# Attention and MLP in one kernel: the subtraction of a weight's low words one step later, the copy of the reciprocals at a step's end

## The chip, the cores and the metric

The kernel runs on one core of one Trainium2 chip. A core has engines that run side by side, each with its own order of instructions: TensorE (PE: matrix products and transposes, into PSUM), VectorE (DVE), ScalarE (ACT), GpSimd (POOL) and SyncE (SP, which here issues transfers). They meet only at semaphores, and an engine does its instructions in the order in which they were written. The metric is the device time of one execution in microseconds (us), as a median of several runs.

## What is computed

Attention over 4 batches, 8 heads, 576 positions and 64 channels, with a bias made from the distance of two positions by a small network, and then a two-layer MLP with a gate on the result. Cut to what matters:

```python
def _attn_ref(q, k, v, w1, b1, w2):
    scores = scale * np.matmul(q, k.transpose(0, 1, 3, 2))
    ...
    h = np.maximum(x @ w1 + b1, 0.0)
    bias = h @ w2
    scores = scores + bias.transpose(2, 0, 1)[None, :, :, :]
    scores = scores - np.max(scores, axis=-1, keepdims=True)
    attn = np.exp(scores)
    attn = attn / (np.sum(attn, axis=-1, keepdims=True) + 1e-09)
    return np.matmul(attn, v).astype(np.float32)

def _moe_ref(x, w_in, w_out):
    h = x @ w_in
    sp = np.where(h > 20.0, h, np.log1p(np.exp(np.minimum(h, 20.0))))
    g = h * np.tanh(sp)
    return (g @ w_out).astype(np.float32)
```

x is 2304 x 512, w_in 512 x 2048 and w_out 2048 x 512. The MLP's weights arrive as 64-bit floating point numbers, two 32-bit words each.

## The kernel before, in words

Three stages follow each other. First the bias is made and written to DRAM (to about 66 us). Then the attention loop, to about 330 us. Then the MLP, to the end.

**The attention loop** goes over 16 pairs of heads (a pair is two heads of one batch), and in each over five chunks of query rows, in the order 0, 1, 4, 2, 3. That makes 80 steps, n = 0 to 79; x = n mod 5 is the step in its pair. Steps 0, 1, 3 and 4 of a pair hold 128 rows of both heads; step 2 holds the last 64 rows of both heads in one tile, and so half the work on DVE and ACT. `step(n)` writes, in this order:

- `scores(n)` (L217, PE): three products for each score tile, for precision (high by high, high by low, low by high). There are two score tiles in PSUM, and a step of 128 rows uses both.
- `add_bias(n)` (L231, DVE): adds the bias to the scores, writes them to SBUF and takes the minimum of the negated row, in one instruction for each score tile; then a short read of the minimum. This frees the score tile. The text calls it the bias-and-minimum.
- `exps(n, 0)` (L246, ACT): the exponential of the first half, with its row sums.
- `transposes(n - 2)`: PE transposes the exponentials of two steps ago into tiles of PSUM (L289, L292), of which there are three in a ring; ACT copies them to SBUF, two main parts (L290) and a tail (L296). Step 1 of a pair also transposes the reciprocals of the sums of the pair before, into the tail's PSUM tile (L295), and `store_reciprocals` copies them to SBUF on DVE (L258) and stores them by SP (L259).
- `exps(n, 1)` (ACT), then `ahead(n)`: loads for later pairs, on SP and POOL.
- `reciprocals` in step 0, for the pair that has just ended (L251, L252, DVE).
- `split(n)`: DVE's side work. In step 2 it splits q and k of the next pair into high and low words (L184). And it prepares one of the MLP's weights, in a cycle of four steps: scale the high word (L112 or L114), shift the low word (L120, which also issues the next load), merge (L127), and put in the sign (L134). With the sign goes `split_weights`: ACT casts the weight to the form that PE takes (L143), and DVE subtracts the cast from the weight for its low words (L144). A cycle of four steps against pairs of five puts the sign in steps 4, 3, 2, 1, 0 in turn; 16 of the 32 weights are prepared so, from n = 6 to n = 69, the rest in the MLP.
- `pv_duo`: parts of the products of the transposed exponentials with v (L322, L326, PE), in one PSUM tile. When a group of rows is done, DVE copies it out (L329: in steps 1 and 3), and the next group's products wait for that copy. SP writes it to DRAM. The text calls L329 the product copy.

No scheduler reorders this: the order of the calls is the order on each engine.

Of the kernel before, what the change touches and what calls it, by code (L numbers as in the profile page):

```python
# [44 lines left out]
def kernel(ctx: ExitStack, tc, qk, v, wb, w2, w_in, w_out, psia, psi4, rinv, eye, out):  # L45
    nc = tc.nc
    pe, dve, act, pool, sp = nc.tensor, nc.vector, nc.scalar, nc.gpsimd, nc.sync
# [39 lines left out]
    todo, w64, half, w32 = list(order), [], [], []  # L87
# [17 lines left out]
    def scale_high(eng):  # L105

        job, w = w64.pop(0)
        high = convp.tile([P, 512], F32, name="high", bufs=1)  # L110
        if eng is act:
            act.mul(high, w.bitcast(F32)[:, :, 1], 2.0 ** -112)  # L112
        else:
            dve.tensor_scalar(high, w.bitcast(F32)[:, :, 1], 2.0 ** -112, None, op0=ALU.mult)  # L114
        half.append((job, w, high))
# [15 lines left out]
    def sign():  # L131
        job, high, c = half.pop(0)
        cu = c.bitcast(U32)
        dve.scalar_tensor_tensor(cu, high.bitcast(U32), 0x80000000, cu,  # L134
                                 op0=ALU.bitwise_and, op1=ALU.bitwise_or)
        w32.append((job, c))

    def split_weights(eng):
        job, c = w32.pop(0)
        if job not in w_hi:  # L140
            w_hi[job] = ring.tile([P, 512], F32R, name="wh{}{}{}".format(*job))
            w_lo[job] = ring.tile([P, 512], F32R, name="wl{}{}{}".format(*job))
        act.copy(w_hi[job], c)  # L143
        eng.tensor_tensor(w_lo[job], c, w_hi[job].bitcast(F32), op=ALU.subtract)  # L144


# [34 lines left out]
    def split_qk(i):  # L181

        lo = hip.tile([P, QW], F32R, name="qklo")
        dve.tensor_tensor(lo, qk_raw.pop(i), qk_hi[i].bitcast(F32), op=ALU.subtract)  # L184
        qk_lo[i] = lo
# [22 lines left out]
    def scores(n):  # L208
        i, c = steps[n]
        hi, lo = qk_hi[i], qk_lo[i]  # L210
        live[n] = [s_ps.tile([P, 2, 512], F32, name="s") for _ in range(2 if c < 4 else 1)]
        for k, (stat, mov) in enumerate(((hi, hi), (hi, lo), (lo, hi))):
            for j in range(2):
                for h in range(2 if c < 4 else 1):
                    rows = slice(h * 64, h * 64 + 64) if c < 4 else slice(0, P)
                    k0 = KO + (0 if h else 64) + j * SH
                    pe.matmul(live[n][h][:, j, :SH], stat[rows, c * P:(c + 1) * P], mov[rows, k0:k0 + SH],  # L217
                              start=(k == 0), stop=(k == 2))

    def add_bias(n):  # L220

        i, c = steps[n]
        bt = bias_t[i // B, c]
        m = st.tile([P, 2], F32, name="m")
        if c < 4:
            pt = pp.tile([P, 2 * S], F32, name="pt")
        else:
            pt = p4p.tile([P, 640], F32, name="pt4")[:, :S]
        for u, s in enumerate(live[n]):
            sl = slice(u * S, (u + 1) * S)  # L230
            dve.tensor_tensor_reduce(  # L231
                out=halves(pt[:, sl]), in0=s[:, :, :SH], in1=halves(bt[:, sl]),
                scale=-0.125, scalar=BIG, op0=ALU.add, op1=ALU.min, accum_out=m[:, u:u + 1])
        live[n] = (pt, m)

    def exps(n, u):

        i, c = steps[n]
        if u == 1 and c == 4:
            return  # L240
        if i not in sums:
            sums[i] = st.tile([P, 9], F32, name="sums", bufs=3)
        pt, m = live[n]
        ps = pt[:, u * S:(u + 1) * S]
        k = 4 * u + c if c < 4 else 8
        act.activation(ps, ps, AF.Exp, bias=m[:, u:u + 1], scale=-1.0, accum_out=sums[i][:, k:k + 1])  # L246

    def reciprocals(i):

        r = sums.pop(i)  # L250
        dve.tensor_scalar(r, r, 1e-9, None, op0=ALU.add)  # L251
        dve.reciprocal(r, r)  # L252
        return r

    def store_reciprocals(i, r, tp):
        hp, b = divmod(i, B)
        rt = rt_first.pop() if rt_first else rt_tile()
        dve.tensor_copy(rt, tp[0:9, P:2 * P])  # L258
        sp.dma_start(out=r_d[b][hp], in_=rt)  # L259

    def pt_tiles(grp):
        w = 256 if grp == 0 else 320
        main = ptp.tile([P, 2, 4, w], F32, name=f"main{grp}")
        tail = tails[grp].pop() if tails.get(grp) else tail_tile(grp)
        return main, tail[:, :w]
# [4 lines left out]
    def rt_tile():  # L270
        return xs.tile([9, P], F32, name="rt", bufs=1)
# [4 lines left out]
    def transposes(n):  # L276
        i, c = steps[n]
        pt, m = live.pop(n)
        grp = 0 if c < 2 else 1
        if (i, grp) not in pt_t:  # L280
            pt_t[i, grp] = pt_tiles(grp)
        main, tail = pt_t[i, grp]
        if c < 4:
            off = c * P if grp == 0 else 64 + (c - 2) * P
            for h in range(2):
                tp = t_ps.tile([P, 512], F32, name="tp")
                for k in range(4):
                    c0 = h * 640 + k * P
                    pe.transpose(tp[:, k * P:(k + 1) * P], pt[:, c0:c0 + P], ident)  # L289
                (dve.tensor_copy if n < 2 and h else act.copy)(main[:, h, :, off:off + P], tp.rearrange("p (k q) -> p k q", k=4))  # L290
            tp = t_ps.tile([P, 512], F32, name="tp")
            pe.transpose(tp[:, :P], pt[:, 512:640], ident)  # L292
            r = rc.pop(n, None)
            if r is not None:
                pe.transpose(tp[0:9, P:2 * P], r, ident)  # L295
            act.copy(tail[:, off:off + P], tp[:, :P])  # L296
            if r is not None:
                store_reciprocals(i, r, tp)
        else:
            tp = t_ps.tile([P, 512], F32, name="tp")  # L300
            for k in range(4):
                pe.transpose(tp[:, k * P:(k + 1) * P], pt[:, k * P:(k + 1) * P], ident)
            act.copy(main[:, :, :, 0:64].rearrange("p h k q -> p k h q"),
                     tp.rearrange("p (k h q) -> p k h q", k=4, h=2))
            tp = t_ps.tile([P, 512], F32, name="tp")
            pe.transpose(tp[0:64, P:2 * P], pt[:, 512:S], ident)
            pe.transpose(tp[:, :P], pt[:, S - P:S], ident)
            act.copy(tail[0:64, 0:64], tp[0:64, P:P + 64])
            act.copy(tail[64:128, 0:64], tp[64:128, 64:128])
# [54 lines left out]
    parts = []  # L364
# [22 lines left out]
    def split(n):  # L387

        i, x = divmod(n, 5)
        if (x == 2 or n == 3) and i + 1 < NPAIR:  # L390
            split_qk(i + 1)
        if half:
            parts.pop(0)()
        elif n > 5 and w64[0][0] in order[:HALF]:
            scale_high(act if x == 2 else dve)
            parts.extend((shift_low, merge, lambda: (sign(), split_weights(dve))))

    def step(n):
        i, x = divmod(n, 5)
        late = n == 4  # L400

        def begin():
            if n < NS:
                scores(n)
                add_bias(n)
                exps(n, 0)

        def end():
            if n < NS:
                exps(n, 1)  # L410
                ahead(n)
            if 0 <= n - 1 < NS and (n - 1) % 5 == 4:
                rc[n - 1] = reciprocals((n - 1) // 5)
            if n < NS:
                split(n)


        if not late:
            begin()
        for k in {3: (0, 1)}.get(n, (n - LAG,)):  # L420
            if 0 <= k < NS:
                transposes(k)
        if not late:
            end()

        if late:
            for k in range(5):
                pv_duo(0, 0, k)
        for j, grp, ks in {4: ((i, 0, (0, 1)),), 0: ((i - 1, 0, (2, 3)),), 1: ((i - 1, 0, (4,)),),
                           2: ((i - 1, 1, (0, 1, 2)),), 3: ((i - 1, 1, (3, 4)),)}[x]:  # L430
            if 0 <= j < NPAIR and (j, grp) != (0, 0):
                for k in ks:
                    pv_duo(j, grp, k)
        if late:
            begin()
            end()
# [133 lines left out]
    for n in range(len(SOFT_AT), NS):  # L570
        step(n)
# [143 lines left out]

    fetch(1)
    step(NS)
    split_x(0, XPARTS)
    hidden(*units[0])
    step(NS + 1)  # L720
    step(NS + 2)
    step(NS + 3)
# [7 lines left out]
    for k in range(len(units) + LAG2):  # L730
        on = k % 3 < 2 if k >= FH else k in (0, 2, 4, 6, 7)
        if w32:
            split_weights(dve)
# [84 lines left out]
```

## Time and profile before

| | us |
|---|---|
| median of 3 runs (743.37 to 745.69) | 744.83 |
| the profiled execution | 745.56 |
| its span, first to last instruction | 743.6 |
| PE busy | 703.2 (95%) |
| DVE busy | 516.1 (69%) |
| ACT busy | 466.9 (63%) |
| POOL busy | 16.5 (2%) |

The shares are averages over the three stages. Matmuls are pipelined, so a busy PE is not PE at its peak. Idle time of an engine that is not the bottleneck costs nothing; what counts is where PE stands, and for whom. The mean granted clock of PE is 0.995 of full speed.

### The profile page before, as it was taken

Reading aid. Unit: us, or ns where it says so; the run is one execution under the profiler, and the core shown is the slowest. Engines: PE = TensorE matmul, PEld = TensorE weight load, DVE = VectorE, ACT = ScalarE, POOL = GpSimd, SP = SyncE. Lnnn points to the kernel's source line nnn. Section 1 sums busy time; section 2 is a strip of 40 time slices with the busy share of each in tenths; the row PEclk is TensorE's granted clock in tenths of the full one; section 3 lists DMA queues with packets and bytes.
Section 4 is the critical chain, followed back from the end, with each engine's and each line's share of the span. In section 5 each row is a group of like instructions: output and inputs, shape, how many; then the busy total and the mean of one; then the engine's idle time right before and its main releaser. Section 6 shows DMA issues by size and latency. Waiting matters only on the chain.

```text
span 743.6 us, 12982 instructions
## 1 busy us (share of the span) xinstructions
PE 703.2 (95%) x4880; PEld 534.3 (72%) x4880; DVE 516.1 (69%) x1051; ACT 466.9 (63%) x964; POOL 16.5 (2%) x26
## 2 busy tenths in 40 slices
PE   6898999999999999999999999999999999999997
PEld 3456666666666666656787888888998888888886
DVE  7885667666766766644888888876675666665554
ACT  7985777777877787783565655564554545444443
POOL 1000000000000000110000000000100000000000
PEclk9999999999999999999999999999999999999999
DMA  8989468356654765423123122134105000010001
GB/s 264 281 275 307 127 198 279 110 163 213 224 161 134 223 220 150 136 74 101 34 81 113 58 86 77 37 113 114 58 1 142 0 1 1 0 57 1 0 1 56
DMA packets 46429, 86.85 MB, mean 117 GB/s; under 512 B 13200, under 2 KB 22048, under 8 KB 46368
## 3 DMA queue, kind: packets, MB, share of 16 engines
q1 hardware_dynamic: 43488, 75.32, 32.3%
q0 software_dynamic: 2304, 10.49, 4.6%
q8 instruction: 38, 0.62, 0.4%
q10 hardware_dynamic: 576, 0.22, 0.1%
q14 instruction: 23, 0.19, 0.1%
HBM read 64.56 MB, written 21.45 MB: 116 GB/s over the span
## 4 chain that ended last, share of the span: by engine, by line
PE 73%; ACT 11%; DVE 10%; issue 3%; DMA 2%; SPq 0%; DVEq 0%; ACTq 0%
PE y L662 23%; PE h L617 22%; PE s L217 8%; PE o L322 8%; PE tp L289 5%; PE bps L515 4%; ACT pt L246 4%; ACT main L290 2%; DVE pt L231 2%; PE o L326 1%; DMA xlo<-r_d 1%; DVE x L329 1%; DMA rawqk<-in_qk_dram 1%; ACT whi L143 1%; DVE e L640 1%
## 5 line engine op out<-in xcount | busy, mean ns | idle before, releaser
L246 ACT ACTIVATE pt<-pt,m 128x576 f32<-128x576 f32 x144 | 112.5, 783 | 64.8 <-DVE m L231 64.4
L231 DVE CUSTOM_DVE_ANT_0 pt<-s,bias 128x576 f32<-128x576 f32 x144 | 103.6, 753 | 39.5 <-PE s L217 39.5
L662 PE MATMUL y<-who,ghi 128*128 128x512 f32 x288 | 112.5, 391 | 2.2 <-ACT ghi L641 1.3
L662 PE MATMUL y<-who,glo 128*128 128x512 f32 x288 | 112.4, 390 | 1.1 <-DVE glo L644 1.0
L662 PE MATMUL y<-wlo,ghi 128*128 128x512 f32 x288 | 112.2, 390 | 0.0
L641 ACT CAST ghi<-e 128x512 fp32r<-128x512 f32 x72 | 44.7, 621 | 105.9 <-DVE e L640 102.6
L322 PE MATMUL o<-main,vt 128*64 128x320 f32 (+1 forms) x512 | 75.8, 418 | 12.9 <-DVE x L329 12.9
L617 PE MATMUL h<-xhi,whi 128*128 128x512 f32 (+1 forms) x320 | 79.9, 370 | 1.3 <-ACT xhi L592 1.2
L617 PE MATMUL h<-xhi,wli 128*128 128x512 f32 (+1 forms) x320 | 79.6, 371 | 0.0
L617 PE MATMUL h<-xlo,whi 128*128 128x512 f32 (+1 forms) x320 | 79.4, 370 | 0.0
L644 DVE TENSOR_TENSOR glo<-e,ghi 128x512 fp32r<-128x512 f32 x72 | 49.8, 691 | 42.3 <-ACT ghi L641 42.3
L289 PE MATMUL tp<-ident,pt 128*128 128x128 f32 x512 | 70.2, 280 | 2.3 <-ACT main L290 2.1
L622 ACT ACTIVATE e<-h 128x512 f32<-128x512 f32 x72 | 42.7, 593 | 45.5 <-PE h L617 45.5
L623 DVE TENSOR_SCALAR e<-e 128x512 f32<-128x512 f32 x72 | 30.6, 425 | 55.4 <-ACT e L622 55.4
L290 ACT COPY main<-tp 128x512 f32<-128x512 f32 x126 | 66.9, 581 | 1.0 <-PE tp L289 0.6
L617 PEld LDWEIGHTS h<-xhi,whi 128*128 128x128 f32 x320 | 57.3, 188 | 13.5 <-ACT xhi L592 2.7
L617 PEld LDWEIGHTS h<-xlo,whi 128*128 128x128 f32 x320 | 57.5, 190 | 10.2
L289 PEld LDWEIGHTS tp<-ident,pt 128*128 128x128 f32 x512 | 56.1, 142 | 12.1 <-ACT main L290 4.1
L617 PEld LDWEIGHTS h<-xhi,wli 128*128 128x128 f32 x320 | 57.4, 190 | 10.1
L662 PEld LDWEIGHTS y<-who,ghi 128*128 128x128 f32 x288 | 54.1, 188 | 14.3 <-ACT ghi L641 2.2
L662 PEld LDWEIGHTS y<-who,glo 128*128 128x128 f32 x288 | 54.1, 188 | 13.6 <-DVE glo L644 2.3
L662 PEld LDWEIGHTS y<-wlo,ghi 128*128 128x128 f32 x288 | 54.1, 188 | 10.8
(73 smaller groups left out, 1029.3 us busy)
## 6 DMA issues: line engine op xcount, KB each, us to landing
bias_d<-bt SPq DMA_DIRECT2D x36, 295.5 KB
qkhi<-in_qk_dram POOLq DMA_DIRECT2D x16, 640.0 KB, 5.6
rawqk<-in_qk_dram SPq DMA_DIRECT2D x16, 640.0 KB
w<-in_w_in_dram SPq DMA_DIRECT2D x16, 512.0 KB
w<-in_w_out_dram SPq DMA_DIRECT2D x16, 512.0 KB
vt<-in_v_dram SPq DMA_DIRECT2D x16, 320.0 KB
bias<-bias_d SPq DMA_DIRECT2D x16, 288.0 KB
out_dram<-w SPq DMA_DIRECT2D x17, 256.0 KB
```

What stands on the lines that cost most here:

```text
L217: pe.matmul(live[n][h][:, j, :SH], stat[rows, c * P:(c + 1) * P], mov[rows, k0:k0 + SH], start=(k == 0), stop=(k == 2))
L231: dve.tensor_tensor_reduce(out=halves(pt[:, sl]), in0=s[:, :, :SH], in1=halves(bt[:, sl]), scale=-0.125, scalar=BIG, op0=ALU.add, op1=ALU. ...
L246: act.activation(ps, ps, AF.Exp, bias=m[:, u:u + 1], scale=-1.0, accum_out=sums[i][:, k:k + 1])
L289: pe.transpose(tp[:, k * P:(k + 1) * P], pt[:, c0:c0 + P], ident)
L290: (dve.tensor_copy if n < 2 and h else act.copy)(main[:, h, :, off:off + P], tp.rearrange("p (k q) -> p k q", k=4))
L322: pe.matmul(o[h * 64:h * 64 + 64, :w], vt[:, h, k, :], main[:, h, k, :], start=(k == 0), stop=False, **kw)
L617: pe.matmul(h[:, u * n:(u + 1) * n], w["i", g4, d][:, r * P:(r + 1) * P], x[:, d, :n], start=(k == 0), stop=(k == 11))
L622: act.activation(e, h, AF.Exp)
L623: dve.tensor_scalar(e, e, E20, None, op0=ALU.min)
L641: act.copy(ghi, e)
L644: dve.tensor_tensor(glo, e, ghi.bitcast(F32), op=ALU.subtract)
L662: pe.matmul(ys[blk][t], g[:, c0:c0 + P], w, start=((blk, f) in first and k == 0), stop=((blk, f) in last and k == 2))
```

## The change

`split_weights` is divided into the cast (`cast_weights`) and the subtraction (`lower_weights`). In the attention loop the sign's step now writes the cast alone, and the next step's `split` writes the subtraction ahead of its own weight part. In the MLP both stay together. And `store_reciprocals` is no longer called within `transposes`; the PSUM tile is remembered, and the copy and its store are written at the end of the step's `end()`, behind `split`.

```diff
     def split_weights(eng):
-        job, c = w32.pop(0)
+        cast_weights()
+        lower_weights(eng)
+
+    def cast_weights():
+        job, c = w32[0]
...
         act.copy(w_hi[job], c)
+
+    def lower_weights(eng):
+        job, c = w32.pop(0)
         eng.tensor_tensor(w_lo[job], c, w_hi[job].bitcast(F32), op=ALU.subtract)
...
-    def store_reciprocals(i, r, tp):
+    turned = []
+
+    def store_reciprocals():
+        i, tp = turned.pop()
...
                 pe.transpose(tp[0:9, P:2 * P], r, ident)
+                turned.append((i, tp))
             act.copy(tail[:, off:off + P], tp[:, :P])
-            if r is not None:
-                store_reciprocals(i, r, tp)
...
         if (x == 2 or n == 3) and i + 1 < NPAIR:
             split_qk(i + 1)
+        if w32:
+            lower_weights(dve)
         if half:
             parts.pop(0)()
         elif n > 5 and w64[0][0] in order[:HALF]:
             scale_high(act if x == 2 else dve)
-            parts.extend((shift_low, merge, lambda: (sign(), split_weights(dve))))
+            parts.extend((shift_low, merge, lambda: (sign(), cast_weights())))
...
             if n < NS:
                 split(n)
+            if turned:
+                store_reciprocals()
```

DVE, step 3 of a pair in which a sign falls (w32 is the weight, whi its cast, wli its low words, x the product copied out, pt and m what the bias-and-minimum writes). Before:

```order
L134 SCALAR_TENSOR_TENSOR w32_1563<-high_1475,w32_1563 128x512
L144 TENSOR_TENSOR wli01_120<-w32_1563,whi01_119 128x512
L329 COPY x_1614<-o_1565 128x320
L231 ISA pt_1633,m_1632<-s_1618,bias3_1093 128x576
L231 ISA m_1632 128x1
L231 ISA pt_1633,m_1632<-s_1619,bias3_1093 128x576
L231 ISA m_1632 128x1
L114 TENSOR_SCALAR high_1653<-w64_1340 128x512
```

In the changed kernel:

```order
L134 SCALAR_TENSOR_TENSOR w32_1563<-high_1475,w32_1563 128x512
L338 COPY x_1613<-o_1565 128x320
L238 ISA pt_1632,m_1631<-s_1617,bias3_1093 128x576
L238 ISA m_1631 128x1
L238 ISA pt_1632,m_1631<-s_1618,bias3_1093 128x576
L238 ISA m_1631 128x1
L151 TENSOR_TENSOR wli01_120<-w32_1563,whi01_119 128x512
L114 TENSOR_SCALAR high_1653<-w64_1340 128x512
```

The subtraction has moved from in front of the product copy to behind the next step's bias-and-minimum.

DVE, step 1 of a pair in which a sign falls (rt is the copy of the reciprocals, qklo the split of q and k in step 2). Before:

```order
L258 COPY rt_1983<-tp_1979 9x128
L134 SCALAR_TENSOR_TENSOR w32_1942<-high_1846,w32_1942 128x512
L144 TENSOR_TENSOR wli03_124<-w32_1942,whi03_123 128x512
L329 COPY x_1996<-o_1899 128x256
L231 ISA pt4_2007,m_2006<-s_1999,bias4_1792 128x576
L231 ISA m_2006 128x1
L184 TENSOR_TENSOR qklo_2027<-rawqk_1751,qkhi_1749 128x1280
L231 ISA pt_2053,m_2052<-s_2038,bias2_1842 128x576
```

In the changed kernel:

```order
L134 SCALAR_TENSOR_TENSOR w32_1942<-high_1846,w32_1942 128x512
L268 COPY rt_1990<-tp_1979 9x128
L338 COPY x_1995<-o_1899 128x256
L238 ISA pt4_2006,m_2005<-s_1998,bias4_1792 128x576
L238 ISA m_2005 128x1
L191 TENSOR_TENSOR qklo_2026<-rawqk_1748,qkhi_1746 128x1280
L151 TENSOR_TENSOR wli03_124<-w32_1942,whi03_123 128x512
L238 ISA pt_2053,m_2052<-s_2038,bias2_1841 128x576
```

The copy of the reciprocals now stands behind the sign, and the subtraction behind the split of q and k of the next step.

The orders of PE and of ACT are the same in both kernels. On SP the store of the reciprocals moves behind the loads of q and k, of the weight and of the bias that the same step issues.

## Rows read from the trace of the kernel before

**Rows 1.** Stretches: us, busy PE, PEld, DVE, ACT, POOL, clock, DMA share, GB/s.

```profile
75.35:305.79 230.44, 211.96 (x1782) 146.38 (x1781) 157.83 (x390) 177.34 (x450) 7.25 (x13) 1.00 0.59 185
163.91:181.80 17.89, 16.31 (x137) 11.28 (x137) 12.19 (x31) 13.32 (x34) 0.53 (x1) 1.00 0.66 202
181.80:199.76 17.96, 16.20 (x137) 11.29 (x137) 12.89 (x32) 14.03 (x35) 0.53 (x1) 1.00 0.83 263
305.79:321.66 15.87, 15.87 (x138) 11.13 (x138) 10.23 (x25) 12.98 (x34) 4.12 (x4) 1.00 0.19 53
400.67:743.00 342.33, 339.07 (x1584) 284.20 (x1584) 235.64 (x388) 174.06 (x291) 2.60 (x2) 1.00 0.15 48
```

**Rows 2.** What TensorE waited for, 75.3 to 305.7 us: total us, times, longest us.

```profile
PE o L322 <- DVE x L329: 12.0, 15, 1.8
PE s L217 <- DVE m L231: 5.3, 11, 0.8
PE tp L289 <- ACT main L290: 1.1, 3, 0.4
```

**Rows 3.** What VectorE waited for, 75.3 to 305.7 us.

```profile
DVE rt L258 <- ACT tail L296: 20.1, 13, 1.8
DVE wlo L144 <- ACT who L143: 13.2, 8, 2.1
DVE wli L144 <- ACT whi L143: 10.8, 8, 2.1
```

**Rows 4.** Timeline, a sign in step 3: start us, us, engine, line [idle before <-releaser].

```profile
168.13 0.69 DVE L134 SCALAR_TENSOR_TENSOR w<-high,w 128x512 uint32<-128x512 uint32 x1
...
170.28 0.62 ACT L143 CAST whi<-w 128x512 fp32r<-128x512 f32 x1
...
170.93 0.69 DVE L144 TENSOR_TENSOR wli<-w,whi 128x512 fp32r<-128x512 f32 x1 [2.11 <-ACT whi L143]
171.54 0.48 DVE L329 COPY x<-o 128x320 f32<-128x320 f32 x1
...
172.08 1.08 PE L322 MATMUL o<-main,vt 128*64 128x256 f32 x8 [1.19 <-DVE x L329]
```

**Rows 5.** Timeline, a sign in step 1 of the next pair, and step 2.

```profile
197.12 0.28 DVE L258 COPY rt<-tp 9x128 f32<-9x128 f32 x1 [1.44 <-ACT tail L296]
...
198.68 0.69 DVE L144 TENSOR_TENSOR wli<-w,whi 128x512 fp32r<-128x512 f32 x1 [0.68 <-ACT whi L143]
...
199.76 1.83 PE L322 MATMUL o<-main,vt 128*64 128x320 f32 x12 [1.76 <-DVE x L329]
...
202.62 0.76 DVE L231 CUSTOM_DVE_ANT_0 pt<-s,bias 128x576 f32<-128x576 f32 x1 [0.84 <-PE s L217]
```

**Rows 6.** Timeline of TensorE behind a sign in step 0, and in step 4.

```profile
214.50 0.53 PE L217 MATMUL s<-qkhi 128*128 128x288 f32 x2 [0.77 <-DVE m L231]
...
229.16 0.40 PE L217 MATMUL s<-qkhi 64*128 64x288 f32 x1 [0.46 <-DVE m L231]
229.84 0.53 PE L217 MATMUL s<-qkhi 64*128 64x288 f32 x3 [0.28 <-DVE m L231]
```

**Rows 7.** Timeline, steps 0 and 1 at the end of the unstalled pair.

```profile
314.94 0.76 DVE L231 CUSTOM_DVE_ANT_0 pt<-s,bias 128x576 f32<-128x576 f32 x1 [1.47 <-PE s L217]
...
315.74 0.78 ACT L246 ACTIVATE pt<-pt,m 128x576 f32<-128x576 f32 x1 [0.29 <-DVE m L231]
...
317.97 0.76 DVE L231 CUSTOM_DVE_ANT_0 pt<-s,bias 128x576 f32<-128x576 f32 x1 [1.25 <-PE s L217]
...
318.83 0.78 ACT L246 ACTIVATE pt<-pt,m 128x576 f32<-128x576 f32 x1 [0.19 <-DVE m L231]
...
320.86 0.28 DVE L258 COPY rt<-tp 9x128 f32<-9x128 f32 x1 [1.44 <-ACT tail L296]
321.06 0.40 DVE L329 COPY x<-o 128x256 f32<-128x256 f32 x1
...
321.46 0.27 PE L292 MATMUL tp<-ident,pt 128*128 128x128 f32 x1
```

## The prediction, made before the result was known

> **What bounds the kernel now.** Read the busy time by stretch first [rows 1]. From 400.67 us to the end TensorE (PE) is busy 339.07 of 342.33 us, with full clock: nothing is to be had there, and the change does not touch it. In the attention loop the same table shows slack: from 75.35 to 305.79 us, 13 pairs of heads, PE is busy 211.96 of 230.44 us. One pair takes 17.89 or 17.96 us, but the pair from 305.79 to 321.66 takes 15.87 us, and PE is busy through all of it. That pair's PE work is the same five steps of scores, transposes and products; what it lacks is the preparation of weights. So 15.87 us is what a pair costs when nobody is late, and the reader is to see that VectorE (DVE, 12.19 us a pair) and ScalarE (ACT, 13.32 us) both have room under it.
>
> Second, who PE waits for in those 13 pairs [rows 2]: 12.0 us for the copy of the product out of PSUM (L329), 5.3 us for the bias-and-minimum of the step before (L231, which frees the score buffers), 1.1 us for ACT's copies of the transposes. All three are waits for a late engine, not for an engine that is full. Third, who DVE waits for [rows 3]: 13.2 and 10.8 us for the cast L143 on ACT, 16 times, and 20.1 us for ACT's tail copy in front of the copy of the reciprocals (L258), 13 times. DVE stands still in order behind these while work that PE needs is queued.
>
> Fourth, the places. In chunk step 3 of a pair [rows 4] DVE finishes the sign at 168.8, then stands 2.11 us, since ACT, which has an exponential of the step in front of the cast, starts the cast only at 170.28. The subtraction starts at 170.93, the product copy behind it at 171.54, and PE, which had nothing left, waited 1.19 us for it. In step 1 [rows 5] DVE stands 1.44 us for the tail, copies the reciprocals, does the sign, stands 0.68 us, subtracts, and only then copies the product: PE waited 1.76 us. In steps 0 and 4 [rows 6] the next bias-and-minimum is late behind the subtraction: PE idles 0.77 us in the one, 0.46 and 0.28 us in the other.
>
> **What the change does, part by part.** Nothing is removed or added; PE's and ACT's orders stay as they are. Two things move on DVE.
>
> *The subtraction.* 16 subtractions of 0.69 us go one step later, behind the next step's bias-and-minimum (and behind the split of q and k in step 2). The cast stays where it was on ACT, so by then it is done: DVE stands 2.1 us for it at the longest [rows 3], and in the new order the product copy (0.48 us, [rows 4]) and two bias-and-minimum instructions of 0.76 us [rows 7] lie in between, 2.0 us, without any wait for the scores; in steps without a product copy 1.5 us and the wait for the scores. The 24.0 us of DVE waiting [rows 3] should nearly go. What is next on the path at each of the four kinds of place: in step 3 the product copy runs when PE's product ends, and the 1.19 us go; in step 1 the copy waits for the tail only; in steps 0 and 4 the bias-and-minimum starts as soon as the scores are there.
>
> What the later subtraction can delay: it takes 0.61 us start to start (170.93 to 171.54), and the weight part beside it 0.69 at the most (the sign, [rows 4]), 1.30 us. In the unstalled pair DVE idles 1.47 us before the bias-and-minimum of step 0 and 1.25 us before that of step 1 [rows 7], so this fits, or misses by 0.05 us. The tightest place is step 2, behind the 1.5 us split of q and k: DVE idles 0.84 us there before the next bias-and-minimum [rows 5], and 0.23 us are left. I cost the move itself at nothing; without that cover it would be 0.61 us at 16 places, 9.8 us.
>
> *The copy of the reciprocals.* 0.20 us start to start (320.86 to 321.06, [rows 7]), once a pair, goes behind the weight part of its step. That part (0.69 us at the most) then runs inside the 1.44 us in which DVE stood for the tail, and no longer between the tail and the product copy. In the pairs without a sign in step 1 PE's wait there is what is left of the 12.0 us: 12.0 - 3 x 1.19 - 3 x 1.76 = 3.15 us in 9 pairs, 0.35 each. The unstalled pair shows the order without a part: copy of reciprocals at 320.86, product copy at 321.06 for 0.40 us, done at 321.46, and PE starts its next product at 321.66, where the stretch ends, without idling [rows 1, 7]. SP's store of the reciprocals moves behind the loads of q and k, and of the bias, that the step issues; its readers are loads at the end of the loop, and the loads in front of it come earlier, not later. I cost this at nothing.
>
> **The sum.** By listed idle time the gain is 12.0 + 5.3 + 1.1 = 18.4 us, the lower bound if all of it goes. By pairs it is 230.44 - 13 x 15.87 = 24.1 us, the upper bound: 5.7 us more, because a score group that starts with one buffer free runs slowly and counts as busy (in [rows 6] one matmul starts at 229.16, the next three at 229.84). I go by the pairs, since the unstalled one contains all of a pair's PE work, and take off two things. ACT: the unstalled pair holds no casts. A cast is 0.62 us; ACT idles only 0.19 us before step 1 and 0.29 us before step 0 [rows 7]. A cast at the end of step 0 puts the tail up to 0.43 us late, of which 0.20 us are free (321.46 to 321.66): 0.23 us, 3 times, 0.7 us. And 0.1 us a pair, an estimate for the DVE work (12.19 against 10.23 us) that the unstalled pair lacks: 1.4 us, rounded up. 24.1 - 0.7 - 1.4 = 22.0 us. The profiled execution took 745.56 us (span 743.6 and 2.0 around it), so 723.6; it lies 0.73 us above the median of 744.83, so I predict 722.8.
>
> **A rule against it.** The wait at the product comes back 15 times in the 13 pairs [rows 2], each time in front of a PSUM tile of which there is one. The Trainium skill's page "Perfetto Trace Analysis", section "Optimization Strategy", says that the same gap repeated on the engine that should be full can mean too few buffers. As a mechanism of this kernel that is a rival below: the 12.0 us stay, since one product tile cannot be emptied and filled at once. The unstalled pair, with the same one tile, has no idle time there [rows 1, 7], so the trace speaks against the rule here.
>
> **Rivals.**
> - *ACT becomes the bound.* It is busy 177.34 us in the 13 pairs [rows 1]; in 208 us that is 85%, and its exponentials wait for DVE, its copies for PE. If it never catches up in the light steps, each of the 16 casts stays on the path with 0.62 us: 9.9 us are given back, 745.56 - 24.1 + 9.9 - 0.73 = 730.6. For it: the small idles in [rows 7]. Against: 2.6 us a pair still free at 15.87.
> - *The transfers.* In the pair from 181.80 the DMA share is 0.83 of 17.96 us [rows 1], 14.9 us; in 15.87 us it would be 0.94. By the code three pairs reload the bias tiles so (every fourth but the last). If they stay at 17.96 us, 3 x 2.09 = 6.3 us are lost: 722.8 + 6.3 = 729.1. Against: no wait in [rows 2, 3] names a transfer.
> - *One product tile,* as above: 745.56 - (24.1 - 12.0) - 0.73 = 732.7.
> - *It doesn't do what it says.* Behind a sign, the next bias-and-minimum now waits for a count of ACT itself, which the subtraction did for it before. If that count were the cast of the same step, DVE would stand as it does now: 744.8. The tiles it reuses were last touched by ACT steps earlier, which speaks against.
> - *Slower.* The copy of the reciprocals reads a PSUM tile of the ring of three for the transposes; PE needs it for the third transpose of the next step, 0.3 us after it is freed in the unstalled pair (321.14 against 321.46, [rows 7]). It now has up to 0.69 us of weight part in front of it, in three pairs a subtraction too. From the point where DVE comes to that part over 1.44 - 0.69 = 0.75 us late, PE's transposes wait. If the copy came 1.5 us late in all 15 pairs, PE would lose 15 x 1.2 = 18 us, and the 12.0 us of the product would stay: 745.56 - 12.1 + 18 - 0.73 = 750.7. Against: DVE gets earlier, not later, by the 24.0 us.
>
> **Chances.** Forecast 0.69, ACT 0.17, transfers 0.06, one tile 0.03, no effect 0.03, slower 0.02. The forecast's own range is 720.3 (all 24.1 us, and 0.4 us of spread) to 726.4 (18.4 us). The range for 8 in 10 goes up to ACT's 730.6: 720.3 to 731. A measurement of this kernel can tell about 0.3%, 2.2 us, from no change. Faster by more: the first four, 0.95; within: 0.03; slower: 0.02.
>
> **What would show it.** Right: the pairs between 75 and 285 us take 15.9 to 16.3 us; DVE's wait for the cast falls from 24.0 us to a few us and reappears as its wait for scores; PE's wait for the product copy falls from 12.0 us to under 2; the copy of the reciprocals waits under 1.1 us a time; the part behind the loop keeps its length. Wrong: PE idling for ACT's copies or tails by more than 3 us (ACT), pairs of 17 us every fourth (transfers), waits at the product unchanged (one tile), the bias-and-minimum released by the cast (no effect), or the third transpose released by the copy of the reciprocals (slower).

## The result, and the profile after

| | before | changed kernel |
|---|---|---|
| median, us | 744.97 (743.37 to 745.69, 4 runs) | 721.2 (719.99 to 722.54, 4 runs) |
| ratio | | 0.9684, 95% interval 0.966 to 0.9708 |
| span of the profiled execution, us | 743.6 | 719.7 |
| PE busy, us | 703.2 (95%) | 697.3 (97%) |
| PE's share of the chain that ended last | 73% | 86% |

721.2 us against 722.8 predicted. The lines of the changed kernel lie up to 13 further down: product copy L338 (was L329), bias-and-minimum L238 (L231), exponential L253 (L246), cast L147 (L143), subtraction L151 (L144), sign L134 as before, copy of the reciprocals L268 (L258), tail copy L307 (L296), products with v L331 (L322).

The stretches that answer to [rows 1] (columns as there), the first of them the same 13 pairs, the third the pair that had no stall before:

```profile
75.44:281.62 206.18, 206.18 (x1783) 144.60 (x1782) 157.88 (x389) 177.45 (x450) 6.33 (x12) 1.00 0.63 204
170.59:186.44 15.85, 15.85 (x138) 11.12 (x137) 12.27 (x31) 13.60 (x35) 0.53 (x1) 1.00 0.91 309
281.62:297.47 15.85, 15.85 (x138) 11.12 (x138) 9.25 (x25) 12.91 (x33) 5.05 (x4) 1.00 0.20 56
376.44:719.70 343.26, 339.07 (x1584) 284.28 (x1584) 235.50 (x388) 174.11 (x291) 2.60 (x2) 1.00 0.15 48
```

In the 13 pairs PE is busy 206.18 of 206.18 us. The loop gains 230.44 - 206.18 = 24.26 us, and the span shrank by 743.6 - 719.7 = 23.9, so all of it comes from here; every pair costs 15.84 to 15.89 us. 18.5 us of the gain were idle time of PE in the view; the other 5.8 us had counted as busy (211.96 against 206.18 us, for the same matmuls). From 376.44 us, which answers to 400.67 before, to the end it takes 343.26 us, against 743.6 - 400.67 = 342.9. In place of [rows 2], the view of what PE waited for has no row at all for this stretch. What DVE waited for there, in place of [rows 3] (total us, times, longest):

```profile
DVE pt L238 <- PE s L224: 32.0, 52, 1.1
DVE rt L268 <- ACT tail L307: 11.8, 13, 1.4
DVE x L338 <- PE o L335: 4.1, 10, 0.6
```

The two rows of the cast are gone, 24.0 us; the wait for ACT's tail fell from 20.1 to 11.8 us (1.4 us once, in the step 1 that has no weight part, and at most 1.1 elsewhere). DVE waits more for PE's scores, 32.0 against 25.0 us, which costs nothing, since PE is full.

The place of [rows 4] in another pair, a sign in step 3 (timeline: start us, us, engine, line, idle before and its releaser):

```profile
158.95 0.69 DVE L134 SCALAR_TENSOR_TENSOR w<-high,w 128x512 uint32<-128x512 uint32 x1
...
159.97 0.49 DVE L338 COPY x<-o 128x320 f32<-128x320 f32 x1 [0.33 <-PE o L335]
...
160.95 0.76 DVE L238 CUSTOM_DVE_ANT_0 pt<-s,bias 128x576 f32<-128x576 f32 x1 [0.49 <-PE s L224]
...
161.10 0.62 ACT L147 CAST whi<-w 128x512 fp32r<-128x512 f32 x1
...
161.65 1.08 PE L331 MATMUL o<-main,vt 128*64 128x256 f32 x8
...
162.31 0.69 DVE L151 TENSOR_TENSOR wli<-w,whi 128x512 fp32r<-128x512 f32 x1
```

Behind the sign DVE waits 0.33 us for the product itself and copies it, and PE goes into the next product at 161.65 without idling. The subtraction comes at 162.31, 0.6 us after its cast has ended (161.10 + 0.62). The place of [rows 5], a sign in step 1:

```profile
184.11 0.69 DVE L134 SCALAR_TENSOR_TENSOR w<-high,w 128x512 uint32<-128x512 uint32 x1
...
185.63 0.28 DVE L268 COPY rt<-tp 9x128 f32<-9x128 f32 x1 [0.84 <-ACT tail L307]
185.84 0.40 DVE L338 COPY x<-o 128x256 f32<-128x256 f32 x1
...
186.44 1.83 PE L331 MATMUL o<-main,vt 128*64 128x320 f32 x12
...
188.25 0.67 DVE L151 TENSOR_TENSOR wli<-w,whi 128x512 fp32r<-128x512 f32 x1
...
189.30 0.76 DVE L238 CUSTOM_DVE_ANT_0 pt<-s,bias 128x576 f32<-128x576 f32 x1 [0.38 <-PE s L224]
```

The sign runs while ACT still copies the tail, the reciprocals go when the tail is there, the product copy right behind; PE has no wait where it had 1.76 us. The subtraction stands behind the split of q and k, and 0.38 us are left before the next scores.

### The profile page after: what moved, and what is told of

Read it like the earlier page. It is cut to its first block, busy times and chain, and to the rows that moved or that the text cites. A ratio compares the mean times of both kernels' runs of the same rounds, so it can differ in the third digit from the quotient of the medians.

```text
span 719.7 us, 12986 instructions
## 1 busy us (share of the span) xinstructions
PE 697.3 (97%) x4880; PEld 532.4 (74%) x4880; DVE 515.3 (72%) x1051; ACT 467.2 (65%) x964; POOL 16.5 (2%) x26
## 4 chain that ended last, share of the span: by engine, by line
PE 86%; DVE 7%; ACT 4%; issue 1%; DMA 1%; DVEq 0%; ACTq 0%; SPq 0%
PE y L675 24%; PE h L630 24%; PE s L224 11%; PE o L331 9%; PE tp L299 8%; PE bps L528 5%; PE o L335 2%; PE tp L311 1%; PE tp L302 1%; DVE e L653 1%; DMA rawqk<-in_qk_dram 1%; DVE e L637 1%; DVE e L652 1%; ACT bt L534 1%; DVE w L127 1%
## 5 line engine op out<-in xcount | busy, mean ns | idle before, releaser
L253 ACT ACTIVATE pt<-pt,m 128x576 f32<-128x576 f32 x144 | 112.7, 782 | 40.8 <-DVE m L238 39.6
L238 DVE CUSTOM_DVE_ANT_0 pt<-s,bias 128x576 f32<-128x576 f32 x144 | 103.7, 753 | 47.4 <-PE s L224 47.4
L331 PE MATMUL o<-main,vt 128*64 128x320 f32 (+1 forms) x512 | 75.8, 418 | 0.8 <-DVE x L338 0.8
```

The source lines that it names most:

```text
L238: dve.tensor_tensor_reduce(out=halves(pt[:, sl]), in0=s[:, :, :SH], in1=halves(bt[:, sl]), scale=-0.125, scalar=BIG, op0=ALU.add, op1=ALU. ...
L331: pe.matmul(o[h * 64:h * 64 + 64, :w], vt[:, h, k, :], main[:, h, k, :], start=(k == 0), stop=False, **kw)
```

## The experiments

Each was run beside the kernel before. Medians of whole executions carry about 1.5 us of scatter from the stretches ahead of and behind the loop (last section), so the table also gives the same 13 pairs of the loop, from one execution each: from the start of the first product of step 2 in pair 1 (the one that waits for step 1's product copy) to the same in pair 14.

| kernel | median, us | before, run beside it | 13 pairs, us |
|---|---|---|---|
| before | | 744.29, 743.46 | 230.44 |
| changed | 721.2 | 744.97 | 206.18 |
| changed, again | 720.86 | 743.46 | 206.18 |
| subtraction late only | 725.47 | 744.29 | 212.45 |
| store late only | 741.23 | 744.29 | 226.62 |
| subtraction in its old place, one cycle late | 719.35 | 744.29 | 206.41 |
| subtraction at the end of the sign's step | 735.81 | 744.29 | 221.89 |
| cast twice | 721.92 | 743.46 | 209.05 |
| subtraction twice | 721.04 | 743.46 | 206.53 |
| early words | 717.15 | 743.46 | 206.18 |

**The subtraction late only.** The changed kernel, with the reciprocals copied where they were:

```diff
             act.copy(tail[:, off:off + P], tp[:, :P])
+            if turned:
+                store_reciprocals()
...
-            if turned:
-                store_reciprocals()
```

> Only the subtraction goes one step later; the copy of the reciprocals stays ahead of the weight part of its step. Theory (DVE's place in line is what cost: both moves take a wait from in front of work that PE needs): the waits behind the cast go, but a weight part of 0.34 to 0.63 us stands again between ACT's tail and the product copy in 13 pairs, of which about 0.35 us show on PE, and in three of them the moved subtraction stands there too (0.5 us more each): 721.2 + 13 x 0.35 + 3 x 0.5 = 727 us (725 to 728.5). Rival (the subtraction is all of it, the copy of the reciprocals hides anyway): 721 to 722.5. Rival (the two need each other, since the product copy waits behind whichever is left): above 732.

Measured: 725.47 us, ratio to before 0.9747 (0.9717 to 0.9777). What PE waited for in the loop (here L333 is the product with v, L340 its copy):

```profile
PE o L333 <- DVE x L340: 5.0, 9, 0.9
```

The loss is of the theory's kind and near its size of 6 us (13 x 0.35 + 3 x 0.5): 725.47 - 720.86 = 4.6 us by the medians of two sets of runs, 212.45 - 206.18 = 6.3 us by the loop. But the idle time sits in 9 places, not in 13: six of 0.40 us, behind the merge and the sign, and three of 0.88, where the moved subtraction stands in front as well. Behind a shift of the low words the view lists no wait; those pairs take 16.03 to 16.07 us, 0.2 more than the floor, and 0.12 of it is idle (PE is busy 15.91 of 16.03 us in the first).

**The store late only.**

```diff
-        if w32:
-            lower_weights(dve)
...
-            parts.extend((shift_low, merge, lambda: (sign(), cast_weights())))
+            parts.extend((shift_low, merge, lambda: (sign(), split_weights(dve))))
```

> Only the copy of the reciprocals and its store go to the end of the step; the subtraction stays in the sign's step. Theory: the 0.35 us in front of the product in 9 pairs go, 3.2 us, the waits behind the cast stay: 745.0 - 3.2 = 741.8 us (740.5 to 743). Rival (the copy of the reciprocals is the larger part): under 735. Rival (the copy hides anyway): 744.5 to 745.5.

Measured: 741.23 us, ratio 0.996 (0.9946 to 0.9973), as the theory had it. The waits show something the expectation had not (L302 is the transpose of the tail):

```profile
PE s L224 <- DVE m L238: 5.3, 11, 0.8
PE tp L302 <- DVE rt L268: 4.6, 3, 1.5
PE o L331 <- DVE x L338: 3.8, 4, 1.2
PE tp L299 <- ACT main L300: 1.1, 3, 0.4
```

In the three pairs with a sign in step 1, PE's wait for the product copy has turned into one for the copy of the reciprocals. One of them, in the timeline:

```profile
194.35 0.28 ACT L307 COPY tail<-tp 128x128 f32<-128x128 f32 x1
...
195.93 0.69 DVE L151 TENSOR_TENSOR wli<-w,whi 128x512 fp32r<-128x512 f32 x1 [2.11 <-ACT whi L147]
196.53 0.27 DVE L268 COPY rt<-tp 9x128 f32<-9x128 f32 x1
...
196.95 0.30 PE L302 MATMUL tp<-ident,pt 128*128 128x128 f32 x1 [1.53 <-DVE rt L268]
```

The tail was there at 194.6, but DVE stood 2.11 us for the cast, and PE's third transpose needs the PSUM tile that the reciprocals sit in. This is the mechanism that the prediction's slower rival named: the copy of the reciprocals behind a late DVE. It costs 1.53 us a place. It was absent from the changed kernel because the subtraction had gone. So the two edits need each other in step 1: by the loop the subtraction's move alone gives 18.0 us, the other 3.8, and both 24.26, 2.5 us more than the sum. Pair by pair, only some 0.2 us of that lies in each of the three pairs with a sign in step 1. About 0.6 us lies in each of the three with a sign in step 0, where the subtraction that moves alone lands in front of step 1's product copy (the 0.88 us above).

**The subtraction in its old place, one cycle late.** Right behind the sign, but on the weight that was cast four steps ago:

```diff
-        job, c = w32[0]
+        job, c = w32[-1]
...
-        if w32:
+        if n == 70:
             lower_weights(dve)
...
-            parts.extend((shift_low, merge, lambda: (sign(), cast_weights())))
+            parts.extend((shift_low, merge, lambda: (sign(), cast_weights(), len(w32) > 1 and lower_weights(dve))))
```

> Built on the changed kernel. The subtraction stands in its old place, right behind the sign and ahead of the product copy and the next bias-and-minimum, but it takes the weight that was cast four steps before, so its 0.6 us of work is where it was and nothing is left of its wait. The last one follows in step 70. Theory (the wait cost, not the work): 721.2 plus about 0.4 us in three steps 2, where the split of q and k leaves 0.24 us: 722.3 us (721 to 723.5). Rival (the 0.6 us of DVE work ahead of the product copy and the bias-and-minimum cost, and the move took that away): 16 x 0.61 = 9.8 us above 721.2, 731 us.

Measured: 719.35 us, ratio 0.967 (0.9641 to 0.9699), not to be told from the changed kernel, and below the range that was expected. The loop's 13 pairs (columns as in [rows 1]):

```profile
74.35:280.76 206.41, 206.36 (x1783) 144.61 (x1782) 157.51 (x389) 177.48 (x450) 6.36 (x12) 1.00 0.62 204
```

206.41 us against 206.18, though 15 of the 16 subtractions stand ahead of the product copy or the bias-and-minimum again (the last follows in step 70). The rival's 9.8 us do not come. With the store late only, the subtraction stood in the same place with its wait, and the 13 pairs took 226.62 us: 20.2 us more. What cost was DVE's standing in line for ACT, not the 0.6 us of work.

**The subtraction at the end of the sign's own step.**

```diff
-        if w32:
-            lower_weights(dve)
...
                     pv_duo(j, grp, k)
+        if w32 and n < NS:
+            lower_weights(dve)
```

> Built on the changed kernel. The subtraction stands at the end of the sign's own step: behind the product copy of steps 1 and 3, but still ahead of the next step's bias-and-minimum, and so still with its wait for the cast. Theory (any work of PE's behind the wait pays): the product copies are free, but the bias-and-minimum is late behind all 16 subtractions. Steps 0, 4 and 2 cost what they did, 3 x 1.15 + 4 x 1.04 + 3 x 0.28 = 8.5 us, step 3 now pays at the scores about 1.2 us three times, step 1 about 0.4 three times: 721.2 + 13.3 = 734.5 us (731 to 738). Rival (only the product copy counted, the late bias-and-minimum was a consequence of it): 721 to 724.

Measured: 735.81 us, ratio 0.9883 (0.9851 to 0.9915). What PE waited for in the loop:

```profile
PE s L224 <- DVE m L238: 7.6, 17, 0.8
PE tp L299 <- ACT main L300: 2.1, 6, 0.4
PE o L331 <- DVE x L338: 0.3, 1, 0.3
```

The product's 12.0 us are down to 0.3, and the wait for the score buffers has grown from 5.3 to 7.6 us, in 17 places instead of 11. The loop is 15.7 us longer than in the changed kernel: 9.9 us of it idle, and 5.8 us in PE's busy time (212.00 us). So the wait has to go from in front of the bias-and-minimum too; behind the product copy alone, it still costs most of what it did.

**Each cast twice on ACT.**

```diff
-            parts.extend((shift_low, merge, lambda: (sign(), cast_weights())))
+            parts.extend((shift_low, merge, lambda: (sign(), cast_weights(), act.copy(w_hi[w32[0][0]], w32[0][1]))))
```

> Built on the changed kernel. In the attention loop ACT makes each cast twice, into the same tile, so that 16 more casts stand in its line, 0.51 us each from start to start. Theory (ACT has room everywhere but at the end of step 0, where 0.06 us are left between the product copy and PE's next product): three times 0.45 us, 721.2 + 1.4 = 722.6 us (721 to 724.5), and PE idles at the product only. Rival (ACT is the next bound, as the prediction's first rival had it): 16 x 0.51 = 8.2 us, 729 us.

Measured: 721.92 us, ratio 0.97 (0.9669 to 0.9731). The loop is 2.9 us longer than in the changed kernel, twice the 1.4 that were expected, and a third of the rival's 8.2. The place was named wrongly: PE waits for ACT's main copies, not for the product:

```profile
PE tp L299 <- ACT main L300: 0.7, 3, 0.2
```

Only 0.7 us show as idle. By the pairs, three with a sign in step 0 take 16.47 us (0.6 more each) and four with a sign in step 4 about 16.1 (0.26 more). So ACT has room for the 16 casts as they are, and little beyond in those steps.

**Each subtraction twice on DVE.**

```diff
         if w32:
+            job, c = w32[0]
+            dve.tensor_tensor(w_lo[job], c, w_hi[job].bitcast(F32), op=ALU.subtract)
             lower_weights(dve)
```

> Built on the changed kernel. Each of the 16 moved subtractions is done twice, 0.61 us more of DVE work at its new place. Theory (the new place has room: DVE idles 0.38 us at least before the next bias-and-minimum, and PE is then still busy with transposes and products for longer than the bias-and-minimum takes): 721.2 to 722.5 us. Rival (the place is nearly full, and the move cost something that the gain hid): 16 x 0.61 = 9.8 us or a good part of it, above 725.

Measured: 721.04 us, ratio 0.9685 (0.9657 to 0.9713); the loop 0.35 us longer. 16 x 0.61 = 9.8 us of DVE work went in nearly for nothing: the new place has room.

**A faster version: two weights' words prepared at the loop's end.**

```diff
-        if w32:
+        if w32 and n <= 70:
             lower_weights(dve)
         if half:
             parts.pop(0)()
+        elif 70 <= n < 75:
+            scale_high(act if x == 2 else dve)
+            parts.extend((shift_low, merge, sign))
...
-        on = k % 3 < 2 if k >= FH else k in (0, 2, 4, 6, 7)
+        on = k % 3 < 2 if k >= FH else k in (4, 6, 7)
```

> A version meant to be faster. With PE full in the attention loop, its idle time is left in the passage to the MLP: 5.3 us in six places between 297 and 377 us, three of them (1.07, 0.32 and 1.00 us) behind DVE, which prepares weights there. Steps 70 to 77 of the loop, where DVE has no weight to prepare, now scale, shift, merge and sign the first two of the second sixteen weights; the MLP's units 0 and 2 no longer do (their casts and subtractions stay in the MLP). Theory (DVE's order sets the passage): 1 to 2.4 us less, 719.5 us (718.5 to 720.5). Rival (the passage is set by the reciprocals' transfers and by ACT): 721 to 721.5.

> The changed kernel as it is, on the same chip as the three kernels beside it, to read their differences by: 720 to 722.5 us.

Measured side by side: 717.15 us for this version, ratio to before 0.963 (0.9605 to 0.9656), and 720.86 us for the changed kernel again, 0.9681 (0.9652 to 0.9711). All five runs of this version (716.02 to 717.97 us) lie below all six of the other (718.70 to 722.38 us), and its median lies below the range that was expected. Three of PE's stalls in the passage to the MLP, in the changed kernel again:

```profile
315.11 2.37 PE L331 MATMUL o<-main,vt 128*64 128x320 f32 x16 [0.88 <-DVE x L338]
...
327.47 0.50 PE L675 MATMUL y<-who,ghi 128*128 128x512 f32 x1 [1.02 <-ACT ghi L654]
...
335.53 0.50 PE L675 MATMUL y<-who,glo 128*128 128x512 f32 x1 [1.01 <-DVE glo L657]
```

and in this version (here L678 is the MLP's second product):

```profile
313.73 2.37 PE L331 MATMUL o<-main,vt 128*64 128x320 f32 x16 [0.88 <-DVE x L338]
...
325.57 0.50 PE L678 MATMUL y<-who,ghi 128*128 128x512 f32 x1 [0.54 <-ACT ghi L657]
```

The 1.01 us for the low words of the gate are gone, the 1.02 us before them are 0.54, and a wait for ACT of 0.85 us at the end of the passage (at 374.64 us) is 0.42 (at 370.95 us): 1.9 us in all. From the end of the 13 pairs to the last instruction the profiled executions take 714.1 - 279.96 = 434.1 against 717.9 - 281.36 = 436.5 us, 2.4 us less, the upper end of the gain that was expected. The medians differ by 3.7. The two profiled executions differ by another 1.4 us ahead of the 13 pairs (73.78 against 75.18 us at their start), which the edit does not touch: from 66 us to that start the granted clock was 1.00 in the one and 0.81 in the other. So I count 2.4 us as the edit's.

## Why the prediction was right, point by point

*What bounds.* That one pair in the trace of before ran without a stall gave the floor: 15.87 us, and the 13 pairs came out at 206.18 / 13 = 15.86. That pair lacks more than the preparation of weights, which the prediction does not say: by the code it issues no loads for later pairs either, and its DMA share is 0.19 against 0.66. The pairs that do load took 15.85 us too, so the floor held. The four places each lost their wait. That the cause is the wait and not the work is shown by the subtraction in its old place without its wait; that it had to leave both the product copy and the bias-and-minimum, by the subtraction at the step's end.

*The sum.* The upper bound, 24.1 us, was the right value, and the two deductions were the wrong part: 0.7 us for ACT's late tail and 1.4 us for DVE work that the floor pair lacks. Both measured nothing. So the loop gained 2.3 us more than the 22.0 forecast, inside the range. The 5.7 us by which the upper bound passes the listed idle time were real: PE's busy time in the 13 pairs is 211.96 us before, 211.77 with the store late only and 212.00 with the subtraction at the step's end, but 206.18 us in the changed kernel, 207.04 with the subtraction late only and 206.36 in the old place without the wait. So part of what a late bias-and-minimum costs PE is counted as its busy time. That the scores themselves carry it, as the prediction says, is only in part shown: their matmuls' summed time falls by 3.35 us (72.28 to 68.93). For ACT the term was mis-sized: I set a duration against an idle time. The rows of the changed kernel behind a sign in step 0 show it:

```profile
198.34 0.80 ACT L253 ACTIVATE pt<-pt,m 128x576 f32<-128x576 f32 x1
...
199.11 0.63 ACT L147 CAST who<-w 128x512 fp32r<-128x512 f32 x1
...
199.62 0.79 ACT L253 ACTIVATE pt<-pt,m 128x576 f32<-128x576 f32 x1
...
201.66 0.28 DVE L268 COPY rt<-tp 9x128 f32<-9x128 f32 x1 [0.68 <-ACT tail L307]
201.87 0.40 DVE L338 COPY x<-o 128x256 f32<-128x256 f32 x1
...
202.33 1.03 PE L331 MATMUL o<-main,vt 128*64 128x320 f32 x6
```

ACT goes on 0.51 us after the cast starts (199.11 to 199.62), not 0.62 us: the next instruction starts before the cast's listed time is over. And in the unstalled pair the exponential in front started 1.08 us before the next one (317.75 in the trace of before, 318.83 in [rows 7]), where one takes 0.77 us start to start (198.34 to 199.11 here): 0.31 us were free, not the 0.19 that the row gives as idle. So the tail is 0.51 - 0.31 = 0.20 us late, and the product copy still ends (202.27) 0.06 us before PE needs it. The cast twice then shows that with 0.5 us more it does cost.

*The tightest place.* 0.23 us was predicted to be left in step 2 and 0.38 are. With the subtraction done twice that is overdrawn, and the loop still grows by 0.35 us only: PE has its transposes and products to do meanwhile.

*The reciprocals.* 3.15 us were put on them alone, 3.8 us by the loop; the other 0.7 us are the three places of 1.76 us that became 1.53 us. Here the working was incomplete: I took their move and that of the subtraction to add up, and in step 1 they do not.

*The rivals.* ACT: no wait of PE's names it, so it is ruled out for the changed kernel; the cast done twice shows that it is near. Transfers: in the pair from 170.59 the DMA share is 0.91 and the pair takes 15.85 us, so that rival is out. One product tile: no wait at the product is left, with the one tile. Hence one tile is enough, and the trace does not bear out here the rule that the prediction quotes; whether a second tile would have hidden the wait as well was not tried. No effect: the bias-and-minimum in [rows 4]'s place of the changed kernel is released by the scores. Slower: did not come, but its mechanism is real, 1.53 us a place when the store moves alone.

*The median.* The sum less 0.73 us for the profiled execution stands up: 745.56 - 24.1 - 0.73 = 720.7, against 721.2 measured.

## What to carry to other kernels

An engine that stands in order behind another's result charges the wait to whatever is queued behind it; put one step of other work between producer and consumer, and look whether the work itself costs (here 9.8 us more of it cost 0.35). Look in the trace for a repetition of the loop that happens to lack the suspected work: its length is the floor, once it is clear what else it lacks, and its idle times, taken from start to start and not from durations, tell what will fit. When two such waits stand one behind the other, moving one alone may hand its cost to a third (here a PSUM tile held by a late copy), so test them apart before adding them up.

## What the runs showed of the hardware that was not expected

The loop repeats to 0.05 us a pair from run to run, and the scatter of the whole lies outside it. In two profiled executions of the same changed kernel, PE's granted clock in the passage to the MLP differs (columns as in [rows 1]; the clock is the third number from the right):

```profile
308.00:317.00 9.00, 7.19 (x28) 4.67 (x30) 4.22 (x8) 4.75 (x11) 0.00 (x0) 0.81 0.80 215
```

```profile
308.00:316.00 8.00, 6.38 (x34) 4.10 (x36) 4.20 (x8) 4.46 (x10) 0.00 (x0) 1.00 0.81 237
```

In both, PE had idled 1.22 us for ACT just before (at 308.93 and 308.67 us) and waited again at 316.91 and 315.11 us. In the first the granted clock is 0.81 of full, a mean over 1.2 and 2.4 GHz, and the stretch between those two points takes 7.98 us; in the second the clock is full, and it takes 6.44 us. The start of the loop's first whole pair varies likewise, from 73.29 to 76.94 us over the ten profiled executions, and it goes with the clock granted from 66 us to that start: 1.00 in the three that start by 74.35 us, 0.81 or 0.82 in the six from 74.88 to 75.74, and 0.69 in the one at 76.94. What decides it was not tried.
